# Later token sums in the expert loop, and low parts read last within each group of matmuls

## The chip, the core and the metric

The kernel runs on one core of one Trainium2 chip. Its engines are TensorE (PE in the profile, with its weight loads as PEld), VectorE (DVE), ScalarE (ACT), GpSimd (POOL) and SyncE (SP, which issues nearly all DMAs). Each works through its own instructions in the order in which the program lists them; semaphores join them. The metric is device microseconds of one execution; lower is better.

## The reference

A retention layer feeds a layer of eight experts, each token to one of them, and that feeds a two-matrix layer with an ELU:

```python
ret = (scale * q @ k.T) * Dmat; x = ret @ v           # 4 batches, 8 heads, 576 tokens, 64 wide
expert_idx = argmax(normalized(x) @ normalized(emb).T / tau)   # 2304 tokens, 8 experts
h = np.maximum(x[mask] @ w1[e], 0.0)                  # 512 -> 1024
out[mask] = gate_w[mask, None] * (h @ w2[e])          # 1024 -> 512
h = out @ w_in                                        # 512 -> 2048
g = np.where(h > 0.0, h, np.exp(np.minimum(h, 0.0)) - 1.0)
return g @ w_out                                      # 2048 -> 512
```

## The kernel before

Every matrix that goes into a matmul of the experts and of the last layer is split into a high part (rounded to fp32r, by a cast or an activation on ACT) and a low part (value minus high part, a subtraction on DVE). A product then takes three matmuls, high by high, high by low and low by high, which add into the same PSUM bank. The helper `three` issues them in that order of stationary and moving operands: weight high by data high (L224), weight high by data low (L225), weight low by data high (L226).

There are three stages. The attention stage and the sorting of tokens to experts take the first 125 us. The **expert loop** (L1144 on) has 64 iterations `i`, eight per expert, up to 366 us, and the **last layer** runs from there to the end in 24 units `n` (three blocks of 768 tokens, eight each).

One iteration of the expert loop issues `mm1(i)`, 12 matmuls of a 128-wide slice of w1 with the expert's tokens (`xth`, `xtl`) into the bank `h`; then ACT's `hh` (L879, ReLU of `h`) and DVE's `hl` (L880, the low part of the same); then `mm2(i-1)`, 12 matmuls of w2's slice with `hh` and `hl` of the iteration before, into four banks `acc0` to `acc3`. At an expert's last slice ACT copies the four banks to `ys`, and a DMA stores them to `yd` in DRAM. Beside that each iteration splits one half-megabyte piece of w1 (`ra` into `ha` and `la`, even `i`) or of w2 (`rb` into `hb` and `lb`, odd `i`) for two iterations ahead and issues the next load of it; transposes (`tp`, L853) and splits the next expert's tokens in its second half; and takes two steps (`decode(2)`) of decoding the last layer's weights: DVE's L146, L148, L151 and L154 on `draw`, ACT's square `dsq` (L149) of the same load, then a DMA of the result to `wd` and another load.

At `i = IOVER = 48`, after a branch for tokens over an expert's capacity (its body is not run here), `LY(0)` loads the first block of tokens, `yb`, 1.5 MB, from `yd`. The last layer needs seven matrices made of it. Four come from `sums(0)`, a generator of four DVE subtractions and additions of 128x768 (L1074: one rewrites a part of `yb`, three write `T`); `high(0, k)` and `low_(0, k)` then split matrix `k` (L1080 on ACT, L1086 on DVE). Before the change the four sums come one each in iterations 50 to 53, and the seven splits in 54 to 60. `decode(2)` runs in iterations up to 53. At 61 to 63 come the first unit's weights (`Sa`, `Ha`, `La`, `Hs`, `Ls`).

In the last layer `product` (L1216) issues, for the 128-row halves `kk` of a matrix, the same three matmuls each, and `unit` (L1291) the same for `fi`.

The schedule is by hand: an engine's order is that of the code. Engine orders below name tiles with a running number behind them.

Of the kernel before, what the change touches and what calls it, by code (L numbers as in the profile page):

```python
# [17 lines left out]
P = 128  # L18
# [11 lines left out]
KD = DM // P  # L30
# [49 lines left out]
def tile_kernel(ctx: ExitStack, tc: tile.TileContext, q, k, v, emb, tau, w1, w2, w_in, w_out, const, out):  # L80
    nc = tc.nc
# [26 lines left out]
    first = cp.tile([P, 1], I32, name="first")  # L108
# [9 lines left out]
    NQ = F2 // P // 2  # L118
# [93 lines left out]
    def tiles_a(i):  # L212

        o = (i % 2) * P
        return [tuple(t[:, kk * 256 + o:kk * 256 + o + P] for t in wa[i // 2]) for kk in range(KD)]

    def tiles_b(i):
        o = (i % 2) * 512
        return [tuple(t[:, o + d * P:o + d * P + P] for t in wb[i // 2]) for d in range(KD)]

    def three(o, l, r, first, last):

        (lh, ll), (rh, rl) = l, r
        nc.tensor.matmul(o, lh, rh, start=first, stop=False)  # L224
        nc.tensor.matmul(o, lh, rl, start=False, stop=False)  # L225
        nc.tensor.matmul(o, ll, rh, start=False, stop=last)  # L226

    tc_manual = ctx.enter_context(tc.manual_schedule())

# [314 lines left out]
    t = ps.tile([P, 512], F32, tag="sc0", name="warm0")  # L544
# [18 lines left out]
    t = ps.tile([P, 512], F32, tag="sc1", name="warm1")  # L563
# [99 lines left out]
    last = range(GROUPS[-1][0], NT)  # L663
# [78 lines left out]
    hi = gt[NG - 1]["hi"]  # L742
# [27 lines left out]
    fi = finish(pid, 0, 2, ids, ids0)  # L770
# [22 lines left out]
    def local(key):  # L793
        return over["pool"] if key == "x" else mp
# [4 lines left out]
    def cap(key):  # L799
        return CH if key == "x" else CAPS[key]  # L800
# [63 lines left out]
    hs = {}  # L864

    def mm1(i, key, w):
        hp = pm.tile([P, 512], F32, tag="h", name=f"h{i}", bufs=2)
        xh, xl = xt[key]
        c = cap(key)
        if i:  # L870
            for kk in range(KD):
                three(hp[:, :c], w[kk], (xh[:, kk, :], xl[:, kk, :]), kk == 0, kk == KD - 1)
        else:
            for l, r in ((0, xh), (1, xh), (0, xl)):
                for kk in range(KD):
                    nc.tensor.matmul(hp[:, :c], w[kk][l], r[:, kk, :], start=l == 0 and r is xh and kk == 0, stop=r is xl and kk == KD - 1)
        hh = local(key).tile([P, CAPS[0]], F32R, tag="hh", name=f"hh{i}")[:, :c]
        hl = local(key).tile([P, CAPS[0]], F32R, tag="hl", name=f"hl{i}")[:, :c]
        nc.scalar.activation(out=hh, in_=hp[:, :c], func=AF.Relu)  # L879
        vec.scalar_tensor_tensor(out=hl, in0=hp[:, :c], scalar=0.0, in1=hh.bitcast(F32), op0=ALU.max, op1=ALU.subtract)  # L880
        hs[i] = (hh, hl)

    acc = {}

    def mm2(i, f, key, w, ra):
        c = cap(key)
        if f == 0:
            for d in range(KD):
                acc[d] = pm.tile([P, 512], F32, tag=f"acc{d}", name=f"acc{i}_{d}")
        for d in range(KD):  # L890
            three(acc[d][:, :c], w[d], hs[i], f == 0, f == 7)
        if f == 7:
            ys = local(key).tile([P, KD, c], F32, tag="ys", name=f"ys{key}", bufs=1)
            for d in range(KD):
                nc.scalar.copy(out=ys[:, d, :], in_=acc[d][:, :c])
            nc.sync.dma_start(out=yd[:, :, bass.ds(ra(), c)], in_=ys)
# [116 lines left out]
    NI1 = NE * 8  # L1013
    IOVER = 48
# [62 lines left out]
    def high(b, k_):  # L1077
        n_ = USE[k_]
        hi, lo = (tp_["pool"].tile([P, 2, HB], F32R, tag="t" + x, name=f"{n_}{x}_{b}", bufs=10) for x in "hl")
        nc.scalar.copy(out=hi, in_=mats[b]["raw"][n_])  # L1080
        mats[b][n_] = (hi, lo)

    def low_(b, k_):
        n_ = USE[k_]
        hi, lo = mats[b][n_]
        vec.tensor_tensor(out=lo, in0=mats[b]["raw"][n_], in1=hi.bitcast(F32), op=ALU.subtract)  # L1086
# [49 lines left out]
    t = pm.tile([P, 512], F32, tag="acc1", name="warmx")  # L1136
# [7 lines left out]
    for i in range(NI1 + 1):  # L1144
        if i == IOVER - 1:
            tc.mark_branch_hint_location("rest", hint="LikelyTaken", engines=ENGS)
        if i < NI1 and i != IOVER:
            mm1(i, i // 8, tiles_a(i))
        if i:
            e, f = divmod(i - 1, 8)  # L1150
            ap = offi[0:1, e:e + 1]
            mm2(i - 1, f, e, tiles_b(i - 1), reg(nc.sync, ap, N) if e else lambda: 0)
        if i == IOVER:
            mm1(i, i // 8, tiles_a(i))
            qctx.close()
            overflow(n_trips)
            tp_["pool"] = ctx.enter_context(tc.tile_pool(name="tpool", bufs=1, side="right"))
            decode(2)
        if i == 0:
            for _ in pick(gslp, gsl):  # L1160
                pass
            gather_expert(1)
        e, f = divmod(i, 8)
        if i < NI1:
            if f == 0 and e:
                gather_expert(e + 1)
            if 4 <= f < 7:
                xpose(e + 1, f - 4)
            if 3 <= f < 6 and e + 1 < NE:
                weighs[e + 1](f - 3)  # L1170
        if i == 9:
            posf = compact()
        if 9 <= i < 21 and i % 4 == 1:
            compact_part((i - 9) // 4, posf)
        if i in (26, 27, 28):
            compact_sum(i - 26)
        if i == 28:
            compact_end()
        if i == 29:
            compact_store()  # L1180
            rest = rest_table(ord_["off"], ord_["cnp"])
        if 30 <= i < 46 and i % 2 == 0:
            next(rest, None)
        if i == 46:
            n_trips = nc.values_load(trips[0:1, 0:1], min_val=0, max_val=NK)
        if i < NI1 - 2:
            (split_b if i % 2 else split_a)(i // 2 + 1)
        if i == IOVER:
            LY(0)
            prep = sums(0)  # L1190
        if IOVER + 1 < i < IOVER + 6:
            next(prep)
        if IOVER + 6 <= i < IOVER + 13:
            high(0, i - IOVER - 6)
            low_(0, i - IOVER - 6)
        elif i < NI1 - 3 and i != IOVER - 1:
            decode(2)
        if i == NI1 - 3:
            Sa(0)
        if i == NI1 - 2:  # L1200
            Ha(0)
            La(0)
            LA(2)
        if i == NI1 - 1:
            Hs(0)
            Ls(0)
            Sa(1)
# [6 lines left out]
    acc6 = {}  # L1214

    def product(n, o, first, sl, m):  # L1216
        b = n // NQ
        hi, lo = (qa if sl in slots_a else qs)["q", n]
        o0 = (slots_a[sl] if sl in slots_a else slots_s[sl]) * 256
        mh, ml = mats[b][m]  # L1220
        for kk in range(2):
            c = slice(o0 + kk * P, o0 + kk * P + P)
            for j, (l, r) in enumerate(((hi[:, c], mh[:, kk, :]), (hi[:, c], ml[:, kk, :]), (lo[:, c], mh[:, kk, :]))):
                nc.tensor.matmul(o, l, r, start=first and kk == 0 and j == 0, stop=kk == 1 and j == 2, skip_group_check=True)  # L1224

    PR = {"P1": ("X", True, "A11", "B11"), "P6": ("Y", True, "S2", "T2"), "P2": ("X", False, "A12", "B21"), "P7": ("Y", False, "S3", "T3"),
          "P5": ("X", True, "S1", "T1"), "P4": ("Y", False, "A22", "T4"), "P3": ("X", False, "S4", "B22")}
# [63 lines left out]
    def unit():  # L1291
        if not units:
            return
        n, z, tt = units.pop(0)
        b, q_ = divmod(n, NQ)
        t = tt + 3 * (z == "B")
        if q_ == 0:
            tag = f"acc{t}" if t < 4 else "tp"
            acc6[t] = pm.tile([P, 512], F32, tag=tag, name=f"o{b}_{t}", bufs=1 if t < 4 else 2)
        bh, bl = qb["q", n]  # L1300
        gh, gl = Q[n]["gh" + z], Q[n]["gl" + z]
        for fi in range(2):
            sl, c = slice(tt * P, (tt + 1) * P), slice(fi * 512, (fi + 1) * 512)
            three(acc6[t], (gh[:, fi, sl], gl[:, fi, sl]), (bh[:, c], bl[:, c]), q_ == 0 and fi == 0, q_ == NQ - 1 and fi == 1)
        if q_ == NQ - 1:
            o_ = dec.tile([P, DM], F32 if t % 2 else I32, tag="dsq" if t % 2 else "db1", name=f"ob{b}_{t}", bufs=2)
            ob = o_ if t % 2 else o_.bitcast(F32)
            if b == 2 and t % 2:
                vec.tensor_copy(out=ob, in_=acc6[t])
            else:  # L1310
                nc.scalar.copy(out=ob, in_=acc6[t])  # L1311
            col = b * NTB + t
            pool.memset(nil, 0.0)
            ins = pool.indirect_dma_start(  # L1314
                out=out[:, :], out_offset=bass.IndirectOffsetOnAxis(ap=idc[:, col:col + 1], axis=0), in_=ob, in_offset=None)
            tc.declare_no_dep(ins.ins, group="rows", reason="each token's row is written once")
            tc.add_to_no_dep_group("rows", ins.ins)
# [29 lines left out]
    for n in range(2, QL):  # L1347
        b, q_ = divmod(n, NQ)
# [3 lines left out]
        if b < 2 and q_ == 4:  # L1352
            prep = sums(b + 1)
# [48 lines left out]
```

## Time and profile before

| what | value |
|---|---|
| median of 3 runs | 748.74 us (748.15 to 749.7) |
| the profiled execution, its own time | 748.12 us |
| its span, first to last instruction | 746.3 us |
| PE busy, share of the span | 715.5 us, 96% |
| PEld busy | 664.2 us, 89% |
| DVE busy | 577.4 us, 77% |
| ACT busy | 460.5 us, 62% |
| POOL busy | 253.6 us, 34% |

Times in the profile count from the start of the span. A matmul's row gives its start and a duration that overlaps with the following ones, so the pace of a run of matmuls is read from start to start. In brackets behind a row stands how long its engine was idle before it, and what released it. [...]

### The profile page before, as it was taken

The numbers are of one execution on the slowest core, as the hardware profiler recorded it, in microseconds if no ns is written. First come the engines' busy times: TensorE is split into PE (matmuls) and PEld (weight loads), VectorE is DVE, ScalarE is ACT, GpSimd is POOL, SyncE is SP. The second block draws the span as 40 slices with busy tenths as digits, with TensorE's granted clock in tenths as the row PEclk, the third lists the DMA queues.
The fourth block names the chain that finished last, engine by engine and source line by source line (L and its number), as shares of the span: only waits on it lengthen the run. The fifth ranks groups of instructions, "written<-read, shape, count | busy, mean of one in ns | idle before, by whom it ended". The sixth has DMA issues, their size and how long they took to land.

```text
span 746.3 us, 13522 instructions
## 1 busy us (share of the span) xinstructions
PE 715.5 (96%) x4901; PEld 664.2 (89%) x4902; DVE 577.4 (77%) x905; ACT 460.5 (62%) x716; POOL 253.6 (34%) x366
## 2 busy tenths in 40 slices
PE   8999977999999999969999999999999999999996
PEld 7998975999999999859988999989999898999995
DVE  3477767788787898668689889988778998777773
ACT  3564643565665575537576667877666787666562
POOL 4367664139931321000532132244312227211103
PEclk9999999999999999989999999999999999999999
DMA  9999955887898989778424231235222114221012
GB/s 201 232 222 236 249 164 155 267 261 262 289 310 282 323 271 325 248 267 249 139 88 138 75 96 58 84 113 171 83 72 71 57 56 164 77 71 58 28 29 84
DMA packets 126747, 123.63 MB, mean 166 GB/s; under 512 B 61738, under 2 KB 96846, under 8 KB 126678
## 3 DMA queue, kind: packets, MB, share of 16 engines
q1 hardware_dynamic: 122390, 111.67, 50.4%
q0 software_dynamic: 3104, 9.83, 3.9%
q10 hardware_dynamic: 1184, 1.24, 0.6%
q8 instruction: 39, 0.64, 0.4%
q14 instruction: 30, 0.25, 0.1%
HBM read 99.88 MB, written 22.85 MB: 164 GB/s over the span
## 4 chain that ended last, share of the span: by engine, by line
PE 25%; issue 20%; POOL 6%; DVE 4%; DMA 1%; ACT 1%; SPq 0%; POOLq 0%; DVEq 0%; ACTq 0%
PE X L1224 6%; PE Y L1224 4%; PE o L226 3%; PE o L224 3%; PE o L225 3%; POOL out_dram L1314 1%; POOL qs L1115 1%; POOL qs L1112 1%; POOL qs L1114 1%; POOL qa L1113 1%; PE acc L225 1%; DMA rb<-in_moe_w_dram 1%; PE acc L226 1%; PE acc L224 1%; PE h L224 1%
## 5 line engine op out<-in xcount | busy, mean ns | idle before, releaser
L1112 POOL TENSOR_TENSOR qs<-qa 128x256 f32<-128x256 f32 x24 | 22.4, 934 | 256.8 <-DMA qa<-wd 55.4
L225 PE MATMUL acc<-hl,hb 128*128 128x342 f32 (+7 forms) x256 | 79.0, 308 | 10.2 <-DVE hl L880 10.2
L224 PE MATMUL h<-xth,ha 128*128 128x332 f32 (+7 forms) x252 | 78.5, 312 | 1.0 <-DVEq L1022 1.0
L226 PE MATMUL acc<-hh,lb 128*128 128x342 f32 (+7 forms) x256 | 78.1, 305 | 0.0
L224 PE MATMUL acc<-hh,hb 128*128 128x342 f32 (+7 forms) x256 | 78.1, 305 | 0.0
L226 PE MATMUL h<-xth,la 128*128 128x332 f32 (+7 forms) x252 | 76.3, 303 | 0.3 <-DVE la L199 0.3
L225 PE MATMUL h<-xtl,ha 128*128 128x332 f32 (+7 forms) x252 | 76.4, 303 | 0.0
L225 PEld LDWEIGHTS acc<-hl,hb 128*128 128x128 f32 x256 | 48.8, 190 | 11.9 <-DVE hl L880 11.9
L879 ACT ACTIVATE hh<-h 128x342 fp32r<-128x342 f32 (+7 forms) x64 | 27.0, 421 | 52.3 <-PE h L226 52.0
L1266 ACT ACTIVATE rA<-hA 128x768 f32<-128x768 f32 x24 | 20.4, 848 | 55.8 <-DVE hA L1259 55.8
L1251 DVE TENSOR_TENSOR u<-Y,m 128x384 f32<-128x384 f32 x48 | 26.6, 554 | 31.6 <-PE Y L1224 29.6
L199 DVE TENSOR_TENSOR lb<-rb,hb 128x1024 fp32r<-128x1024 f32 x32 | 39.8, 1245 | 13.0 <-ACT hb L194 13.0
L199 DVE TENSOR_TENSOR la<-ra,ha 128x1024 fp32r<-128x1024 f32 x32 | 39.7, 1240 | 12.3 <-ACT ha L194 12.2
L224 PEld LDWEIGHTS h<-xth,ha 128*128 128x128 f32 x252 | 47.5, 189 | 1.6 <-DVEq L1022 1.3
L226 PEld LDWEIGHTS acc<-hh,lb 128*128 128x128 f32 x256 | 48.9, 191 | 0.0
L224 PEld LDWEIGHTS acc<-hh,hb 128*128 128x128 f32 x256 | 48.6, 190 | 0.0
L226 PEld LDWEIGHTS h<-xth,la 128*128 128x128 f32 x252 | 47.5, 189 | 0.6 <-DVE la L199 0.5
L819 POOL DMA_INDIRECT row<-xd,idsp x21 | 21.6, 1029 | 76.6 <-ACT xth L858 74.3
L225 PEld LDWEIGHTS h<-xtl,ha 128*128 128x128 f32 x252 | 47.6, 189 | 0.0
L1314 POOL DMA_INDIRECT out_dram<-ob,idc x18 | 20.3, 1127 | 68.4 <-ACT ob L1311 65.9
L194 ACT CAST hb<-rb 128x1024 fp32r<-128x1024 f32 x32 | 33.3, 1041 | 3.5 <-issue 2.2
L1259 DVE TENSOR_TENSOR hB<-X,u 128x384 f32<-128x384 f32 x48 | 26.5, 553 | 10.7 <-PE X L1224 10.4
(1684 smaller groups left out, 2390.1 us busy)
## 6 DMA issues: line engine op xcount, KB each, us to landing
ra<-in_moe_w_dram SPq DMA_DIRECT2D x31, 512.0 KB
rb<-in_moe_w_dram SPq DMA_DIRECT2D x31, 512.0 KB
qb<-wd SPq DMA_DIRECT2D x48, 256.0 KB
draw<-in_moe_w_in_dram SPq DMA_DIRECT2D x16, 512.0 KB
draw<-in_moe_w_out_dram SPq DMA_DIRECT2D x16, 512.0 KB
wd<-db SPq DMA_DIRECT2D x32, 256.0 KB
qa<-wd SPq DMA_DIRECT2D x24, 256.0 KB
qa<-wd SPq DMA_DIRECT2D x48, 128.0 KB
```

The source lines that it names most:

```text
L194: nc.scalar.copy(out=hi, in_=src)
L199: nc.vector.tensor_tensor(out=lo, in0=src, in1=hi.bitcast(F32), op=ALU.subtract)
L224: nc.tensor.matmul(o, lh, rh, start=first, stop=False)
L225: nc.tensor.matmul(o, lh, rl, start=False, stop=False)
L226: nc.tensor.matmul(o, ll, rh, start=False, stop=last)
L819: pool.indirect_dma_start(out=t[:m].rearrange("p k w -> p (k w)"), out_offset=None, in_=xd[:, :], in_offset=bass.IndirectOffsetOnAxis(ap=i ...
L879: nc.scalar.activation(out=hh, in_=hp[:, :c], func=AF.Relu)
L1112: pool.tensor_tensor(out=S1, in0=A21, in1=A22, op=ALU.add)
L1224: nc.tensor.matmul(o, l, r, start=first and kk == 0 and j == 0, stop=kk == 1 and j == 2, skip_group_check=True)
L1251: vec.tensor_tensor(out=S_[nm], in0=S_["Y"], in1=S_["m1"], op=ALU.add)
L1259: vec.tensor_tensor(out=half(n, z)[:, fi, :], in0=Q[n][bank], in1=Q[n][term], op=ALU.add)
L1314: ins = pool.indirect_dma_start(out=out[:, :], out_offset=bass.IndirectOffsetOnAxis(ap=idc[:, col:col + 1], axis=0), in_=ob, in_offset=None)
```

## The change

Two things change, and no arithmetic is added or removed.

First, within a group of matmuls that add into the same place those that read a low part made by DVE come last. `three` is gone. A new helper `several` takes all pairs of a group and issues first, for each pair, weight high with data high and weight high with data low, and behind them all the matmuls with the low weights. It serves `mm1` (whose moving low part `xtl` is old; `la` is the fresh one), `product` and `unit`. `mm2` is written out: for each `d` the high and low weights with `hh`, and behind these eight the four with `hl`. `mm1(0)` is as before.

Second, `sums(0)` comes in iterations 54 and 55, two steps each, and the seven splits come in 56 to 62. `LY(0)` and `decode` stay where they are.

```diff
-    def three(o, l, r, first, last):
-        (lh, ll), (rh, rl) = l, r
-        nc.tensor.matmul(o, lh, rh, start=first, stop=False)
-        nc.tensor.matmul(o, lh, rl, start=False, stop=False)
-        nc.tensor.matmul(o, ll, rh, start=False, stop=last)
+    def several(o, ops, first, last):
+        seq = [(lh, r) for (lh, _), rr in ops for r in rr] + [(ll, rh) for (_, ll), (rh, _) in ops]
+        for n_, (l, r) in enumerate(seq):
+            nc.tensor.matmul(o, l, r, start=first and n_ == 0, stop=last and n_ == len(seq) - 1, skip_group_check=True)
...
-            for kk in range(KD):
-                three(hp[:, :c], w[kk], (xh[:, kk, :], xl[:, kk, :]), kk == 0, kk == KD - 1)
+            several(hp[:, :c], [(w[kk], (xh[:, kk, :], xl[:, kk, :])) for kk in range(KD)], True, True)
...
+        hh, hl = hs[i]
         for d in range(KD):
-            three(acc[d][:, :c], w[d], hs[i], f == 0, f == 7)
+            for w_ in range(2):
+                nc.tensor.matmul(acc[d][:, :c], w[d][w_], hh, start=f == 0 and w_ == 0, stop=False)
+        for d in range(KD):
+            nc.tensor.matmul(acc[d][:, :c], w[d][0], hl, start=False, stop=f == 7)
...
-        if IOVER + 1 < i < IOVER + 6:
+        if i in (IOVER + 6, IOVER + 7):
             next(prep)
-        if IOVER + 6 <= i < IOVER + 13:
-            high(0, i - IOVER - 6)
-            low_(0, i - IOVER - 6)
-        elif i < NI1 - 3 and i != IOVER - 1:
+            next(prep)
+        elif IOVER + 8 <= i < IOVER + 15:
+            high(0, i - IOVER - 8)
+            low_(0, i - IOVER - 8)
+        elif i < IOVER + 6 and i != IOVER - 1:
             decode(2)
```

`product` and `unit` call `several` with their two halves in the same way.

On DVE, iterations 50 to 52 before the change: the first sum (`yb`, L1074) stands between the split of `la` and the next decode step, ahead of two low parts `hl`.

```order
L199 TENSOR_TENSOR la_5484<-ra_4842,ha_5483 128x1024
L1074 TENSOR_TENSOR yb_5394<-yb_5394 128x2x384
L146 TENSOR_SCALAR db_5503<-draw_5370 128x512
L148 SCALAR_TENSOR_TENSOR db_5503<-draw_5370,db_5503 128x512
L880 SCALAR_TENSOR_TENSOR hl_5521<-h_5507,hh_5520 128x282
L199 TENSOR_TENSOR lb_5538<-rb_4896,hb_5537 128x1024
L1074 TENSOR_TENSOR T_0_5498<-yb_5394 128x768
L151 SCALAR_TENSOR_TENSOR db_5503<-draw_5370,db_5503 128x512
L154 SCALAR_TENSOR_TENSOR db_5503<-dsq_5502,db_5503 128x512
L880 SCALAR_TENSOR_TENSOR hl_5572<-h_5558,hh_5571 128x282
```

On DVE after the change the sums stand two by two behind the splits of iterations 54 and 55:

```order
L199 TENSOR_TENSOR la_5706<-ra_5496,ha_5705 128x1024
L1076 TENSOR_TENSOR yb_5394<-yb_5394 128x2x384
L1076 TENSOR_TENSOR T_0_5720<-yb_5394 128x768
L878 SCALAR_TENSOR_TENSOR hl_5739<-h_5725,hh_5738 128x282
L199 TENSOR_TENSOR lb_5755<-rb_5546,hb_5754 128x1024
L1076 TENSOR_TENSOR T_0_5721<-yb_5394,T_0_5720 128x768
L1076 TENSOR_TENSOR T_0_5722<-yb_5394,T_0_5720 128x768
L878 SCALAR_TENSOR_TENSOR hl_5785<-h_5771,hh_5784 128x276
```

The first sum has moved behind all remaining decode steps and behind the splits and low parts of four iterations.

On PE, the group `mm2` of one iteration before the change reads `hl` in every third matmul, from the second on:

```order
L224 MATMUL acc_0_5418<-hh_4938,hb_4883 128x282
L225 MATMUL acc_0_5418<-hl_4939,hb_4883 128x282
L226 MATMUL acc_0_5418<-hh_4938,lb_4884 128x282
L224 MATMUL acc_1_5419<-hh_4938,hb_4883 128x282
L225 MATMUL acc_1_5419<-hl_4939,hb_4883 128x282
```

After it, the end of the next such group is

```order
L891 MATMUL acc_2_5420<-hh_5414,lb_4884 128x282
L891 MATMUL acc_3_5421<-hh_5414,hb_4883 128x282
L891 MATMUL acc_3_5421<-hh_5414,lb_4884 128x282
L893 MATMUL acc_0_5418<-hl_5415,hb_4883 128x282
L893 MATMUL acc_1_5419<-hl_5415,hb_4883 128x282
L893 MATMUL acc_2_5420<-hl_5415,hb_4883 128x282
L893 MATMUL acc_3_5421<-hl_5415,hb_4883 128x282
```

`hl` is read from the ninth matmul on, and the four banks are complete only with the last four.

## Rows read from the trace of the kernel before

**Rows 1.** Page, part 1: engine, busy us (share of the span), instructions.

```profile
PE 715.5 (96%) x4901; PEld 664.2 (89%) x4902; DVE 577.4 (77%) x905; ACT 460.5 (62%) x716; POOL 253.6 (34%) x366
```

**Rows 2.** Waits, whole span: engine line, waited for: us in total, times, longest.

```profile
ACT hh L879 <- PE h L226: 52.0, 33, 2.5
...
PE acc L225 <- DVE hl L880: 10.2, 7, 6.8
```

**Rows 3.** Waits of PE from 125 to 310 us.

```profile
PE acc L225 <- DVE hl L880: 2.6, 4, 0.8
...
PE h L226 <- DVE la L199: 0.3, 1, 0.3
```

**Rows 4.** Timeline of PE at 300: start, us, engine, line, operation [idle before <-releaser].

```profile
300.61 0.29 PE L224 MATMUL acc<-hh,hb 128*128 128x292 f32 x1
301.67 0.40 PE L225 MATMUL acc<-hl,hb 128*128 128x292 f32 x1 [0.77 <-DVE hl L880]
301.92 0.30 PE L226 MATMUL acc<-hh,lb 128*128 128x292 f32 x1
```

**Rows 5.** Timeline of PE, 314 to 347.

```profile
314.04 0.30 PE L224 MATMUL acc<-hh,hb 128*128 128x282 f32 x1
...
315.62 0.30 PE L224 MATMUL h<-xth,ha 128*128 128x282 f32 x1
...
317.20 0.29 PE L224 MATMUL acc<-hh,hb 128*128 128x282 f32 x1
...
324.26 0.60 PE L225 MATMUL acc<-hl,hb 128*128 128x282 f32 x1 [6.77 <-DVE hl L880]
...
326.77 0.44 PE L226 MATMUL acc<-hh,lb 128*128 128x282 f32 x1
...
330.83 0.60 PE L853 MATMUL tp<-ident,row 128*128 128x128 f32 x4
331.19 0.37 PE L224 MATMUL h<-xth,ha 128*128 128x282 f32 x1
...
347.17 0.29 PE L224 MATMUL acc<-hh,hb 128*128 128x276 f32 x1
```

**Rows 6.** Timeline of DVE, 312 to 327.

```profile
312.80 1.21 DVE L199 TENSOR_TENSOR la<-ra,ha 128x1024 fp32r<-128x1024 f32 x1
321.82 0.96 DVE L1074 TENSOR_TENSOR yb<-yb 128x768 f32<-128x768 f32 x1 [7.81 <-DMA rb<-in_moe_w_dram]
...
323.76 0.45 DVE L880 SCALAR_TENSOR_TENSOR hl<-h,hh 128x282 fp32r<-128x282 f32 x1
324.12 1.22 DVE L199 TENSOR_TENSOR lb<-rb,hb 128x1024 fp32r<-128x1024 f32 x1
325.25 0.95 DVE L1074 TENSOR_TENSOR T<-yb 128x768 f32<-128x768 f32 x1
326.12 0.68 DVE L151 SCALAR_TENSOR_TENSOR db<-draw,db 128x512 int32<-128x512 int32 x1
326.84 0.69 DVE L154 SCALAR_TENSOR_TENSOR db<-dsq,db 128x512 f32<-128x512 f32 x1
```

**Rows 7.** Windows: stretch, us, busy of each engine, PEclk, DMA share, GB/s.

```profile
324.00:325.00 1.00, 0.74 (x3) 0.74 (x4) 1.00 (x2) 0.00 (x0) 0.00 (x0) 0.50 1.06 382
325.00:326.00 1.00, 1.00 (x6) 1.00 (x5) 1.00 (x2) 0.00 (x0) 0.00 (x0) 0.50 0.46 159
```

**Rows 8.** Timeline of SP: its DMA issues, 313 to 316.

```profile
313.26 0.65 SPq L1063 DMA_DIRECT2D yb<-yd  x1
314.73 0.39 SPq L173 DMA_DIRECT2D rb<-in_moe_w_dram  x1
315.17 0.52 SPq L132 DMA_DIRECT2D draw<-in_moe_w_in_dram  x1
```

**Rows 9.** Timeline of ACT, 314 to 318.

```profile
314.91 0.67 ACT L149 ACTIVATE dsq<-draw 128x512 f32<-128x512 f32 x1 [2.50 <-DMA draw<-in_moe_w_in_dram]
315.48 0.39 ACT L879 ACTIVATE hh<-h 128x282 fp32r<-128x282 f32 x1
```

More of the change, by code (lines that the diff above doesn't have):

```diff
@@ L1220, in product @@
         mh, ml = mats[b][m]
[L1221 to L1224, printed above, removed]
+        cs = [slice(o0 + kk * P, o0 + kk * P + P) for kk in range(2)]
+        several(o, [((hi[:, c], lo[:, c]), (mh[:, kk, :], ml[:, kk, :])) for kk, c in enumerate(cs)], first, True)
     PR = {"P1": ("X", True, "A11", "B11"), "P6": ("Y", True, "S2", "T2"), "P2": ("X", False, "A12", "B21"), "P7": ("Y", False, "S3", "T3"),
@@ L1301, in unit @@
         gh, gl = Q[n]["gh" + z], Q[n]["gl" + z]
-        for fi in range(2):
-            sl, c = slice(tt * P, (tt + 1) * P), slice(fi * 512, (fi + 1) * 512)
-            three(acc6[t], (gh[:, fi, sl], gl[:, fi, sl]), (bh[:, c], bl[:, c]), q_ == 0 and fi == 0, q_ == NQ - 1 and fi == 1)
+        sl = slice(tt * P, (tt + 1) * P)
+        several(acc6[t], [((gh[:, fi, sl], gl[:, fi, sl]), (bh[:, fi * 512:(fi + 1) * 512], bl[:, fi * 512:(fi + 1) * 512])) for fi in range(2)],
+                q_ == 0, q_ == NQ - 1)
         if q_ == NQ - 1:
```

## The prediction

> **What bounds the kernel now.** I read the page's busy shares first. PE is busy 96% of the span [rows 1], so the end is set by PE's work and by the gaps in it, and this change takes no matmul away. Next the waits of the whole span: PE's largest entry by far is the low part `hl` made by DVE, 10.2 us in seven waits, one of them 6.8 us [rows 2]. Four of the seven, 2.6 us, lie before 310 us, with one wait of 0.3 us for `la` [rows 3]. The other direction is longer: ACT waited 52.0 us for PE's bank `h` [rows 2]. ACT and DVE follow PE in the expert loop, so PE time won there is not lost again to a slower engine.
>
> Then the long wait, on three engines. DVE ends the split `la` at 314.0 and stands idle for 7.81 us before the first sum [rows 6]. The releaser is given as the load of `rb`, but the sum reads `yb`; `yb` was issued at 313.26 and `rb` right behind it [rows 8], and the two are not told apart there. Behind the sum stand, in DVE's order, the decode steps and `hl`, which starts at 323.76 [rows 6]. PE reaches the group `mm2` that reads this `hl` at 317.20, gets one matmul out, and resumes at 324.26 [rows 5]. [...]
>
> **The early waits.** The example [rows 4] shows what one costs. The second matmul starts 1.06 us after the first, where the undisturbed pace is about 0.13 (twelve matmuls in 1.58 us [rows 5]): 0.93 us lost, and the next start comes 0.25 after it instead of 0.13, so 1.05 us in all. The idle column gives 0.77 for it. The difference, 0.28, is the overlap of a matmul's row with its follower and the restart. [...] By the idle column alone this term would be 2.9 us.
>
> From start to start the five early waits are 2.6 + 0.3 + 5 x 0.28 = 4.3 us. The new order makes `hl` due at the ninth matmul of the group instead of the second, seven matmuls or 0.93 us later, and `la` at the ninth instead of the third, 0.8 us later. The four waits for `hl` average 0.65 idle and the example, the longest, is just covered. I take 4.2 us; the lower end is 2.9.
>
> **The long wait.** Between 317.20 and 347.17 [rows 5] pass 29.97 us. In them lie twelve groups of twelve matmuls (`mm2` of iterations 51 to 56, `mm1` of 53 to 58). Eight are 282 columns wide at 1.58 us [rows 5]; four are 276 wide, which scales to 1.55. With three transpose groups of 0.36 (330.83 to 331.19 [rows 5]) that is 12.6 + 6.2 + 1.1 = 19.9 us of work. So 10.1 us are lost here: 6.93 at the wait (7.06 from start to start, less 0.13), some 1.3 at half clock (ten matmuls take 2.51 us from 324.26 to 326.77 [rows 5] instead of 1.3, and the first few later ones), and the rest in two later waits for `hl`, behind further sums. With the sums in iterations 54 and 55 `yb` has long landed and DVE passes from `la` straight to the decode step; the `hl` that came at 323.76 needs only `hh`, which ended near 315.9 [rows 9], and a `draw` that had landed by 314.91 [rows 9]; it comes near 316.5, before PE asks at 317.3, even without the new order.
>
> What is late next? Two things, and they are costs of this term.
>
> The **load behind `yb`**. The decode load `draw` of 315.17 is queued behind `yb` and `rb` [rows 8]. The transfers are saturated until 325 and thin out in the next microsecond [rows 7]. That `draw` lands between 323.2 (0.5 MB behind the landing of `rb` or `yb` near 321.8, at 382 GB/s [rows 6, 7]) and 325.4. Before the change nobody met it: everyone stood still. Now ACT's next `dsq` waits for it, and in ACT's order `hh` of iteration 53 stands behind that `dsq`. From the landing it takes 0.57 (start of `dsq` to start of `hh` [rows 9]) plus 0.4. PE has four groups of 1.58 and two transposes of 0.36 to do from 317.20 before it asks for that `hh`, which is 324.25. Landing at 324.3, the middle, gives `hh` at 325.4 and a wait of 1.15 us. The ends are 0 and 2.3.
>
> The **sums in their new place**. In iterations 54 and 55 DVE does, from start to start, two splits at 1.13, four sums at 0.87 to 0.95, the last two decode steps (0.72 + 0.6) and two `hl` at 0.36 [rows 6], about 8.1 us, against 2 x 3.16 = 6.3 of PE [rows 5]. It falls 1.8 behind, of which the new order covers 0.93: 0.85 us lost. The ends are 0 and 1.8, as if there were no cover. From 56 on DVE has a split, a low part and `hl`, 2.4 us for 3.1 of PE, and recovers.
>
> So this term is 10.1 - 1.15 - 0.85 = 8.1 us, between 6.0 and 10.1.
>
> **What I cost at nothing.** The seven splits end in iteration 62 instead of 60; their first reader is the last layer, and the load of the first unit's weights moves up with the loop. Behind 366 us the waits view names no low part for PE, so the order in `product` and `unit` wins nothing. An expert's four banks are now complete with the ninth to twelfth matmul instead of the third to twelfth, so ACT's copies to `ys` begin 0.8 us later, once per expert. ACT has the room (52.0 us of waiting [rows 2]) and the next use of the banks lies a whole `mm1`, 1.6 us or more, behind; without that cover it would be up to 0.8 us in each of eight experts. The pace of a matmul by its neighbours: a group `mm2`, with four banks, takes 314.04 to 315.62, and `mm1`, with one bank, 315.62 to 317.20 [rows 5], the same within 0.01 us in twelve, or 1 ns each. The change reorders some 3,400 matmuls (756 + 768 in the loop, 1,008 + 864 in the last layer), so 1 ns each would be 3.4 us either way; I take 0.
>
> **The sum.** 4.2 + 8.1 = 12.3 us. Against the profiled execution, 748.12, that is 735.8; this execution lies 0.6 below the median of the runs, 748.74, so I forecast 736.4. The ends of the terms give 8.9 to 14.4, that is 739.8 to 734.3.
>
> **The rivals.** First, **the wait is handed on**: the loads behind `yb` come at the late end or later, ACT stands at `dsq` or at the cast of `rb`, the later `ys` copies push ACT further, and the sums in 54 and 55 find DVE already late. Then the second term is 6.0 less some 2 to 3 for an ACT that stays behind over an expert's end, and the first is 2.9: a gain of 6 to 7, near 742. For it speaks the saturated stretch [rows 7]; against it that at most the one `draw` is due before 326. [...] 14%.
>
> Second, **the change misses the cause**: the first sum waits not for `yb` but for something that also comes late in iteration 54, as the named releaser `rb` would allow. The 7.8 us then come back there, softened by 0.9 of cover: a gain of 4.2 + 1.5, near 743. Against it: `rb` of 314.73 is itself split in iteration 53, ahead of the sum's new place. 4%.
>
> Third, **slower**: repeated stationary operands. Before, each group of three starts with two matmuls on the same weights; in `mm2` now no two neighbours share them. If a load of new weights showed between matmuls, 4 of 12 matmuls in 64 groups, 256, would pay. A weight load's row is busier than the matmul pace leaves room for (664.2 us for 4,902, 0.136 us each [rows 1], against 0.132). The loss must pass 12.3 / 256 = 48 ns each to decide; at 60 ns it is 15.4 us and the time 751.8. Against it: in each group before, the third matmul already changes the weights, and it starts no later than the second (a whole group of twelve keeps 0.132 [rows 5]). 4%.
>
> **How the numbers follow.** The forecast has 74%: 736.4, with 733.5 to 740 for its bounds and a little for the pace. Handed on 14%, cause missed 4%, slower 4%, and 4% for a gain above 15 us, where PE running ahead also removes stalls that the idle column hides. To leave out no more than 2 in 10 the range takes in the forecast and the larger part of the first rival: 733.5 to 741.5. A measurement of this kernel can tell about 0.2%, 1.5 us, from no change. Faster by more than that: 0.92; within it 0.04 (parts of the second rival and of the first, with a pace lost in the last layer); slower 0.04.
>
> **What would show it.** In the profile after: no wait of PE above 3 us in the expert loop and PEclk at 1.00 through the stretch around 310 to 340; DVE's first sum with no wait for a DMA; a new wait of ACT's `dsq` for `draw` of about 3 us, and of PE for `hh` of about 1; waits for `hl` below 1 us in total; a start of the last layer about 12 us earlier, and the same length of it. It is wrong if the last layer becomes longer (pace), if PE still waits several us for `hl` (cause), or if the early waits reappear under the name of `hh` or `lb`.

## The result and the profile after

The kernel after the change takes 740.91 us (median of 4 runs, 739.2 to 742.63) against 749.22 for the kernel before in the same comparison (4 runs, 748.15 to 750.05): a ratio of 0.989, with an interval from 0.986 to 0.992. That is 8.3 us; the forecast was 12.3 us and 736.4, with a range up to 741.5. The profiled execution after took 739.2 us with a span of 737.4, 8.9 us shorter than the span before.

The busy shares answer to [rows 1], and the second row, of the waits view, to the 52.0 us of [rows 2]: PE's work is what it was, and ACT waits 10 us less for `h`.

```profile
PE 714.9 (97%) x4902; PEld 662.6 (90%) x4902; DVE 579.2 (79%) x905; ACT 458.5 (62%) x716; POOL 255.3 (35%) x366
```

```profile
ACT hh L877 <- PE h L225: 42.4, 32, 2.3
```

Then the waits of PE in the expert loop. This is the waits view of PE over the whole span after (engine line, waited for: us in total, times, longest); the entries left out lie before the loop, at its edges or, one of 0.7, in the last layer.

```profile
PE acc L891 <- ACT hh L877: 2.2, 2, 2.0
...
PE h L225 <- DVEq L1024: 1.0, 1, 1.0
...
PE acc L891 <- DVE lb L199: 0.3, 1, 0.3
```

The 10.2 us for `hl` [rows 2] and the early waits [rows 3] are gone; 0.3 us of them came back under the name of `lb`. New is a wait for `hh`, 2.2 us. The timeline of PE shows where. First two rows of before that stand nowhere above (the restart at the branch of iteration 48, the last layer's first matmul):

```profile
306.04 0.40 PE L224 MATMUL h<-xth,ha 128*128 128x282 f32 x1 [1.04 <-DVEq L1022]
365.51 0.34 PE L1224 MATMUL X<-B11h,ha('q', 0)_6083 128*128 128x384 f32 x1
```

The same places after, and between them the first matmul of `mm2` in iterations 51 to 54 and 57 (314.53 answers to 317.20 and 338.00 to 347.17 of [rows 5]):

```profile
302.97 0.40 PE L225 MATMUL h<-xth,ha 128*128 128x282 f32 x1 [1.04 <-DVEq L1024]
314.53 0.40 PE L891 MATMUL acc<-hh,hb 128*128 128x282 f32 x1 [0.26 <-ACT hh L877]
318.45 0.29 PE L891 MATMUL acc<-hh,hb 128*128 128x282 f32 x1
324.17 0.40 PE L891 MATMUL acc<-hh,hb 128*128 128x282 f32 x1 [1.97 <-ACT hh L877]
328.24 0.29 PE L891 MATMUL acc<-hh,hb 128*128 128x282 f32 x1
338.00 0.29 PE L891 MATMUL acc<-hh,hb 128*128 128x276 f32 x1
356.59 0.34 PE L225 MATMUL X<-B11h,ha('q', 0)_6083 128*128 128x384 f32 x1
```

From these starts the 8.9 us can be divided by stretch:

The loop's first matmul started at 122.68 before and at 123.08 after; work ahead of the loop is the same in both.

| stretch | before, us | after, us | gain | forecast |
|---|---|---|---|---|
| to the loop's first matmul | 122.68 | 123.08 | -0.40 | 0 |
| to the restart at the branch | 183.36 | 179.89 | 3.47 | 4.2 |
| to `mm2` of iteration 51 | 11.16 | 11.56 | -0.40 | 0 |
| to `mm2` of iteration 57 | 29.97 | 23.47 | 6.50 | 8.1 |
| to the last layer | 18.34 | 18.59 | -0.25 | 0 |
| the last layer, to the span's end | 380.8 | 380.8 | 0 | 0 |

The sums no longer wait for anything, and the clock stays up. The first is DVE's first sum after (it answers to 321.82 in [rows 6]); the second a part of the windows (stretch, us, busy of PE, PEld, DVE, ACT, POOL, then PEclk, the clock granted to TensorE as a share of full speed, DMA share, GB/s).

```profile
330.28 0.95 DVE L1076 TENSOR_TENSOR yb<-yb 128x768 f32<-128x768 f32 x1
```

```profile
308.00:310.00 2.00, 2.00 (x17) 2.00 (x16) 1.97 (x5) 1.33 (x2) 0.00 (x0) 1.00 0.00 0
312.00:314.00 2.00, 2.00 (x18) 2.00 (x16) 0.00 (x0) 0.48 (x1) 0.00 (x0) 1.00 1.02 353
324.00:326.00 2.00, 1.82 (x12) 1.58 (x12) 1.97 (x4) 2.00 (x4) 0.00 (x0) 1.00 1.06 406
```

PEclk is 1.00 where it was 0.50 before [rows 7]. The DMA column tells something new: the transfers are empty at 308 to 310 (share 0.00) and full from 312 on (1.02 and more up to 328). What PE now waits for is on ACT and SP:

```profile
313.52 0.67 ACT L149 ACTIVATE dsq<-draw 128x512 f32<-128x512 f32 x1 [4.19 <-DMA draw<-in_moe_w_in_dram]
323.16 0.66 ACT L149 ACTIVATE dsq<-draw 128x512 f32<-128x512 f32 x1 [3.94 <-DMA draw<-in_moe_w_in_dram]
323.72 0.39 ACT L877 ACTIVATE hh<-h 128x282 fp32r<-128x282 f32 x1
```

```profile
309.37 0.41 SPq L132 DMA_DIRECT2D draw<-in_moe_w_in_dram  x1
311.94 0.65 SPq L1065 DMA_DIRECT2D yb<-yd  x1
...
313.85 0.75 SPq L132 DMA_DIRECT2D draw<-in_moe_w_in_dram  x1
```

The `draw` issued at 313.85, behind `yb`, is used at 323.16, the moment it lands; `hh` of iteration 53 stands behind its square on ACT; PE resumes 0.45 after `hh` began. The mechanism is the one forecast. Its price is not.

### The profile page after: what moved, and what is told of

It reads as the page before. It is cut to its first block, busy times and chain, and to the rows that moved or that the text cites. A ratio compares the mean times of both kernels' runs of the same rounds, so it can differ in the third digit from the quotient of the medians.

```text
span 737.4 us, 13518 instructions
## 1 busy us (share of the span) xinstructions
PE 714.9 (97%) x4902; PEld 662.6 (90%) x4902; DVE 579.2 (79%) x905; ACT 458.5 (62%) x716; POOL 255.3 (35%) x366
## 4 chain that ended last, share of the span: by engine, by line
PE 35%; issue 9%; DVE 8%; ACT 2%; DMA 2%; POOL 1%; POOLq 0%; SPq 0%; ACTq 0%; DVEq 0%
PE o L225 16%; PE X L225 9%; PE Y L225 7%; PE h L225 1%; PE acc L891 1%; DMA ra<-in_moe_w_dram 1%; PE acc L893 1%; POOL out_dram L1315 1%; DVE hA L1280 1%; DVE glA L1288 1%; DVE xA L1277 1%; DMA draw<-in_moe_w_in_dram 1%; DVE hB L1280 0%; DVE la L199 0%; DVE xB L1277 0%
## 5 line engine op out<-in xcount | busy, mean ns | idle before, releaser
L891 PE MATMUL acc<-hh,hb 128*128 128x342 f32 (+7 forms) x256 | 73.7, 304 | 2.2 <-ACT hh L877 2.2
L225 PE MATMUL h<-xth,ha 128*128 128x332 f32 (+7 forms) x252 | 74.3, 311 | 1.0 <-DVEq L1024 1.0
L891 PE MATMUL acc<-hh,lb 128*128 128x342 f32 (+7 forms) x256 | 73.6, 303 | 0.3 <-DVE lb L199 0.3
L225 PE MATMUL h<-xtl,ha 128*128 128x332 f32 (+7 forms) x252 | 72.2, 303 | 0.0
L199 DVE TENSOR_TENSOR la<-ra,ha 128x1024 fp32r<-128x1024 f32 x32 | 39.1, 1222 | 11.6 <-ACT ha L194 11.5
L893 PE MATMUL acc<-hl,hb 128*128 128x342 f32 (+7 forms) x256 | 47.1, 306 | 0.1
L225 PE MATMUL h<-xth,la 128*128 128x332 f32 (+7 forms) x252 | 45.6, 303 | 0.0
L893 PEld LDWEIGHTS acc<-hl,hb 128*128 128x128 f32 x256 | 38.8, 188 | 1.4 <-DVE hl L878 1.0
L225 PEld LDWEIGHTS h<-xth,la 128*128 128x128 f32 x252 | 38.5, 189 | 0.0
L1260 DVE TENSOR_TENSOR hB<-X,u 128x384 f32<-128x384 f32 x48 | 26.6, 553 | 10.7 <-PE X L225 10.4
```

Of the source, the lines that this page charges most:

```text
L199: nc.vector.tensor_tensor(out=lo, in0=src, in1=hi.bitcast(F32), op=ALU.subtract)
L225: nc.tensor.matmul(o, l, r, start=first and n_ == 0, stop=last and n_ == len(seq) - 1, skip_group_check=True)
L891: nc.tensor.matmul(acc[d][:, :c], w[d][w_], hh, start=f == 0 and w_ == 0, stop=False)
L893: nc.tensor.matmul(acc[d][:, :c], w[d][0], hl, start=False, stop=f == 7)
L1260: vec.tensor_tensor(out=half(n, z)[:, fi, :], in0=Q[n][bank], in1=Q[n][term], op=ALU.add)
```

## Experiments

All ratios are against the kernel before in the same comparison; its medians there were 749.0 to 749.7.

**The two parts apart.** One kernel has only the moved sums, one only the new order.

```diff
 # e1_sums_only: the kernel before, with
-        if IOVER + 1 < i < IOVER + 6:
+        if i in (IOVER + 6, IOVER + 7):
+            next(prep)
             next(prep)
-        if IOVER + 6 <= i < IOVER + 13:
+        elif IOVER + 8 <= i < IOVER + 15:
...
```

> The kernel before with the four sums moved to iterations 54 and 55 and the splits to 56 to 62, every matmul in its old order. My theory (the sums' place removes the 6.8 us wait, the order of the matmuls removes the small early ones): the five early waits for hl and la stay (2.9 us idle), the long one is gone and PEclk stays at 1.00 near 310 to 340; in its place ACT waits some 3 us for draw, PE about 1 us for hh of iteration 53, and hl is late in 54 to 56 by up to 1.8 us in all since nothing covers it. Gain 6 to 8 us, near 742. Rival (the whole gain of 8.3 us comes with the order of the matmuls): no gain, near 749.

Measured: 743.6 us (740.39 to 745.89, 6 runs), ratio 0.9913 (0.9893 to 0.9934), a gain of 6.1. The moved sums find `yb` landed; PE (first row) and ACT (second) show what came instead, and the windows the clock behind it:

```profile
328.30 0.55 PE L224 MATMUL acc<-hh,hb 128*128 128x282 f32 x1 [2.72 <-ACT hh L879]
```

```profile
327.29 0.66 ACT L149 ACTIVATE dsq<-draw 128x512 f32<-128x512 f32 x1 [4.69 <-DMA draw<-in_moe_w_in_dram]
```

```profile
328.00:330.00 2.00, 0.94 (x2) 0.63 (x3) 1.93 (x4) 2.00 (x4) 0.00 (x0) 0.60 1.04 398
330.00:332.00 2.00, 2.00 (x10) 2.00 (x10) 1.86 (x3) 0.56 (x2) 0.00 (x0) 0.50 0.60 214
```

The wait for the `draw` behind `yb` belongs to the moved sums; it needs no early gain. It is longer than forecast, and behind it the clock falls here, which was not expected. The profiled execution, 745.89 us, is the longest of the six.

```diff
 # e2_order_only: the changed kernel, with
-        if i in (IOVER + 6, IOVER + 7):
-            next(prep)
+        if IOVER + 1 < i < IOVER + 6:
             next(prep)
-        elif IOVER + 8 <= i < IOVER + 15:
+        if IOVER + 6 <= i < IOVER + 13:
...
```

> The changed kernel with the four sums back in iterations 50 to 53 and the splits in 54 to 60, every matmul in its new order. My theory: PE has gained 3.5 us at the start of iteration 49, but SP's issue of yb after the branch moves up by only 1.3 us and DVE still stands until yb lands, so most of the lead is lost at the long wait, which becomes longer in idle time (about 8 us less 0.9 of cover); the two hl waits behind it go (1.3 us). Gain 3 to 4 us, near 745.5. Rival (the two parts add up, each on its own path): the gain is that of the whole less that of the sums alone, and the long wait stays at 6 us or below.

Measured: 745.58 us (743.61 to 746.22, 6 runs), ratio 0.9942 (0.9926 to 0.9958), a gain of 4.2, as expected. PE and DVE:

```profile
302.94 0.40 PE L225 MATMUL h<-xth,ha 128*128 128x282 f32 x1 [1.04 <-DVEq L1024]
322.56 1.31 PE L893 MATMUL acc<-hl,hb 128*128 128x282 f32 x4 [7.30 <-DVE hl L878]
```

```profile
320.13 0.96 DVE L1076 TENSOR_TENSOR yb<-yb 128x768 f32<-128x768 f32 x1 [9.21 <-DMA rb<-in_moe_w_dram]
```

PE passes the branch 3.10 us earlier than before (306.04), but `yb` is used only 1.69 earlier (320.13 against 321.82 in [rows 6]). The long wait becomes longer, 7.30 instead of 6.8, although the new order covers seven matmuls more. In this execution, the longest of the six, only 1.92 of the 3.10 us are left at the last layer (363.59). One reason is the clock: PE works at half clock (PEclk 0.50) from 322.56 to about 328.2, before only from 324.26 to about 327.5. The parts gain 6.1 and 4.2 alone, 10.3 together; the whole gains 8.3 to 8.9. The intervals are too wide to tell these sums apart; that the parts share a limit is shown by the rows, where most of the lead is lost at the load.

**The order in the last layer alone.**

```diff
 # e4_last_layer_order: the kernel before, with `several` added and used in `product` and `unit` only
-            for j, (l, r) in enumerate(((hi[:, c], mh[:, kk, :]), (hi[:, c], ml[:, kk, :]), (lo[:, c], mh[:, kk, :]))):
-                nc.tensor.matmul(o, l, r, start=first and kk == 0 and j == 0, stop=kk == 1 and j == 2, skip_group_check=True)
+        several(o, [((hi[:, c], lo[:, c]), (mh[:, kk, :], ml[:, kk, :])) for kk, c in enumerate(cs)], first, True)
...
```

> The kernel before with the new order of matmuls in the last layer alone (product and unit); the expert loop is untouched. My theory: no low part is waited for there and the pace of a matmul does not depend on its neighbours, so no change, within 0.7 us of the kernel before, and the last layer lasts 380.8 us as before. Rival (the order changes the pace, by 1 ns or more on each of 1,872 matmuls): 1.9 us or more to either side.

Measured: 748.89 us (748.03 to 750.04, 11 runs), ratio 0.9991 (0.998 to 1.0003): no difference that can be told. With the equal length of the last layer in the table above, the rival on weight loads and pace falls, there and, by the undisturbed groups of the loop (304.64 to 307.79 for 24 matmuls after, 3.15 us, against 3.16 before), in `mm2` too.

**The load behind the others.** `LY(0)` goes to the end of iteration 49, behind that iteration's `rb` and `draw`.

```diff
 # e3_load_behind: the changed kernel, with
-        if i == IOVER:
-            LY(0)
-            prep = sums(0)
...
+        if i == IOVER + 1:
+            LY(0)
+            prep = sums(0)
```

> The changed kernel with the load yb issued an iteration later, behind the loads of rb and draw of iteration 49 instead of ahead of them; nothing else moves. My theory (what is left of the loss is ACT waiting for a draw that lies behind 1.5 MB of yb): ACT's second wait for draw (3.9 us) and PE's wait of 2.0 us for hh of iteration 53 go, the first one (4.2 us of ACT, 0.3 us of PE) stays, and the first sum still finds yb landed: 2 to 3 us less than the changed kernel, near 738.3. Rival (the loss is DVE's crowd of sums in 54 and 55, or SP's late start after the branch): the wait of PE moves to another name and the time stays within 0.7 us of the changed kernel's.

Measured: 738.13 us (736.37 to 739.8, 5 runs), ratio 0.9849 (0.9829 to 0.987), as expected and better than both kernels. SP, ACT and PE:

```profile
313.36 0.42 SPq L132 DMA_DIRECT2D draw<-in_moe_w_in_dram  x1
...
314.57 0.65 SPq L1065 DMA_DIRECT2D yb<-yd  x1
```

```profile
321.12 0.66 ACT L149 ACTIVATE dsq<-draw 128x512 f32<-128x512 f32 x1 [1.30 <-DMA draw<-in_moe_w_in_dram]
```

```profile
315.15 0.40 PE L891 MATMUL acc<-hh,hb 128*128 128x282 f32 x1 [0.19 <-ACT hh L877]
331.73 0.78 PE L893 MATMUL acc<-hl,hb 128*128 128x282 f32 x4 [0.38 <-DVE hl L878]
```

With `yb` behind it the `draw` lands 7.76 us after its issue instead of 9.31, PE's wait of 1.97 is gone, and `yb`, not needed before iteration 54, is still in time. From the restart (303.65) to the last layer's first matmul (355.52) pass 51.87 us instead of 53.62 in the changed kernel.

**Why the load is late: SP's place or full transfers.** Between the store of `yd` and the next `draw` SP issues nothing for 7.14 us in the changed kernel (302.23 to 309.37), of which it spends 4.9 in the branch of iteration 48. Two kernels leave that branch out.

```diff
 # e8_before_no_branch: the kernel before; e7_after_no_branch: the changed kernel; both with
-            overflow(n_trips)
```

> The kernel before without the branch (left out; its body is not run here). Same theory: yb is issued about 4 us earlier against TensorE, so VectorE's wait at the first sum falls from 7.81 to about 4 us and TensorE's wait for hl from 6.8 to about 3 us, and with a shorter wait the half clock behind it may be gone. Gain 1.04 + 4 and up to 1.3 for the clock: 742.5 to 745. Rival, the load is late by the transfers and not by the issue: the long wait stays at 6 us or more and the time is about 748.

Measured: 746.91 us (745.33 to 748.1, 9 runs), ratio 0.996 (0.9946 to 0.9975), a gain of 2.6. SP, DVE and PE:

```profile
310.86 0.62 SPq L1063 DMA_DIRECT2D yb<-yd  x1
```

```profile
320.35 0.96 DVE L1074 TENSOR_TENSOR yb<-yb 128x768 f32<-128x768 f32 x1 [6.61 <-DMA yb<-yd]
```

```profile
322.79 0.60 PE L225 MATMUL acc<-hl,hb 128*128 128x282 f32 x1 [6.36 <-DVE hl L880]
```

`yb` goes out 2.40 us earlier than at 313.26 [rows 8] and is used 1.47 earlier; PE, free of the branch, comes earlier too, and still waits 6.36 instead of 6.8. So this is nearer to the rival: the issue moved by only 2.40 us, not 4, of which 1.47 came through. The run bears on another point: the sum's releaser is named `yb` here.

> The changed kernel without the branch for tokens over an expert's capacity (left out; its body is not run here). If SyncE's stay of some 4.8 us in that branch is what makes the loads behind it late against TensorE, SP's first draw and the load of yb go out about 4 us earlier against TensorE (yb then has to wait for the store of yd to land, some 6 us), ACT's wait of 3.94 us at the second dsq falls below 1 us, the first one falls too, and TensorE's two waits for hh (0.52 and 2.23 from start to start) go. Together with the 1.04 us that TensorE itself waits at the branch that is a gain of 3.8 us on the changed kernel, about 737.1. Rival, the loads are late because the transfers are full wherever SP issues them: only the 1.04 is won, about 739.9, and TensorE still waits 1.5 to 2 us for hh.

Measured: 735.72 us (735.13 to 736.89, 4 runs), ratio 0.9809 (0.9789 to 0.9829). SP, ACT and PE, and two windows:

```profile
308.24 0.63 SPq L1065 DMA_DIRECT2D yb<-yd  x1
...
310.19 0.49 SPq L132 DMA_DIRECT2D draw<-in_moe_w_in_dram  x1
```

```profile
320.93 0.66 ACT L149 ACTIVATE dsq<-draw 128x512 f32<-128x512 f32 x1 [3.70 <-DMA draw<-in_moe_w_in_dram]
```

```profile
321.93 0.40 PE L891 MATMUL acc<-hh,hb 128*128 128x282 f32 x1 [1.73 <-ACT hh L877]
```

```profile
308.00:310.00 2.00, 2.00 (x18) 2.00 (x17) 1.97 (x4) 0.86 (x3) 0.00 (x0) 1.00 1.09 328
320.00:322.00 2.00, 0.27 (x3) 0.07 (x1) 0.33 (x1) 1.07 (x3) 0.00 (x0) 1.00 1.08 417
```

The `draw` goes out 3.66 us earlier, at 310.19, and is used 2.23 earlier, 10.7 us after its issue instead of 9.3. The hole in the transfers at 308 to 310 is filled and PE's first wait for `hh` gone, as the first theory said; the second wait stays, 1.73 us, as the rival said. By medians the gain on the changed kernel is 5.2, above either figure; by the two profiled spans (737.4 and 735.0) it is 2.4, between them. The two traces are far from typical: one is the shortest of its four runs (739.2 to 742.63), the other the longest (735.13 to 736.89). All four runs without the branch lie below both 737.1 and 739.9, so the time speaks for the first theory and the wait that stays for the rival.

**A queue of its own for `yb`.**

```diff
 # e6_pool_queue: the changed kernel, with
-            nc.sync.dma_start(out=yb, in_=yd[:, :, b * TB:(b + 1) * TB])
+            (nc.sync if b else nc.gpsimd).dma_start(out=yb, in_=yd[:, :, b * TB:(b + 1) * TB])
```

> The changed kernel with the load of yb issued by GpSimd, on a queue of its own, in the same place of the code. Theory (the second draw is late because it is queued behind yb, and yb is late because SP issues it behind its branch): yb goes out as soon as the store of yd has landed, some 3 us earlier; ACT's wait at the second dsq falls from 3.94 to below 2.5 us and TensorE's wait for hh of 1.97 to below 0.5; the first draw now shares the transfers with yb, and TensorE's first wait for hh (0.26) may grow to 1.5. Time 737 to 740. Rival (full transfers, whatever the queue): ACT still waits 4 us or more at one of the two, and the sum of TensorE's waits for hh stays at 2 us or more: 741.

Measured: 741.83 us (741.44 to 742.9, 4 runs), ratio 0.9897 (0.9876 to 0.9918): the rival's case. POOL, ACT and PE:

```profile
309.71 0.82 POOL L1065 DMA_DIRECT2D yb<-yd  x1 [12.60 <-DVE db L154]
```

```profile
324.57 0.66 ACT L149 ACTIVATE dsq<-draw 128x512 f32<-128x512 f32 x1 [2.12 <-DMA draw<-in_moe_w_in_dram]
```

```profile
322.50 0.41 PE L225 MATMUL h<-xth,ha 128*128 128x282 f32 x1 [1.82 <-ACT ha L194]
325.57 0.40 PE L891 MATMUL acc<-hh,hb 128*128 128x282 f32 x1 [1.03 <-ACT hh L877]
```

No longer behind `yb` in a queue, the `draw` of 312.95 lands 11.6 us after its issue, later than in the changed kernel, and `ra`, the load that `ha` is made of, is late as well. So to stand behind `yb` in its queue is not what it takes to be late; to be in flight together with it was enough here (11.62 us against 9.31). `ra`, issued at 310.85 with `yb` already out, is used 10.55 us later; the `ra` of 311.19 in the changed kernel, issued ahead of `yb`, was there when ACT came to it after 7.00.

**More in front of the branch, and `yb` in parts.** Both start from the version with the load behind.

```diff
 # e9_decode_ahead: e3_load_behind, with the two decode steps behind the branch in iteration 47 instead
             overflow(n_trips)
-            decode(2)
...
-        elif i < IOVER + 6 and i != IOVER - 1:
+        elif i < IOVER + 6:
             decode(2)
```

> The changed kernel with the load of yb behind the other loads of iteration 49, and the first two decode steps behind the branch moved to iteration 47, ahead of it, so that the first draw is issued ahead of SP's branch too. Theory: ACT's wait of 4.1 us at the dsq of iteration 50 goes, TensorE's remaining wait for hh (0.2) too; the time falls by at most 0.5 us from 738.1, to 737.6 to 738.1. Rival: the two steps on VectorE ahead of the branch make hl of iteration 48 later and TensorE waits up to 0.5 us more there: 738.6.

Measured: 740.65 us (738.97 to 741.38, 4 runs), ratio 0.9881 (0.986 to 0.9902): no gain, rather a loss of some 2 us, more than the rival said and by another way. PE:

```profile
327.81 0.40 PE L225 MATMUL h<-xth,ha 128*128 128x276 f32 x1 [1.29 <-ACT ha L194]
```

The early wait for `draw` is gone, but PE meets the next late load, `ra`, and later waits 0.66 for `lb`. The loads behind the branch have fallen back against PE: the first of `ra` goes out 8.70 us after PE's restart (302.73 to 311.43) instead of 7.72 in the version with the load behind (303.65 to 311.37).

```diff
 # e10_four_parts: e3_load_behind, LY(0) making the tile only, and
+        if IOVER < i < IOVER + 5:
+            k_ = i - IOVER - 1
+            nc.sync.dma_start(out=tp_["yb"][:, k_, :], in_=yd[:, k_, :TB])
```

> The changed kernel with the load of yb cut into four parts of 384 KB, issued at the ends of iterations 49 to 52, each behind the other loads of its iteration. Theory: the limit is the transfers. The loop by itself asks for one ra, one rb and one draw of 512 KB and one wd of 256 KB in two iterations of some 6.3 us, about 285 GB/s; the trace shows some 390 GB/s when the transfers are full; four parts in 12.6 us add about 125 GB/s, so they just fill them. No load of the loop then stands behind more than one part: ACT's waits for draw stay below 2 us except for the first one behind SP's branch, no wait of TensorE in iterations 50 to 56 is above 0.5 us, the sums find yb landed, and the time is 737 to 738.1, like the version with the whole load behind the others (738.1) or a little better. Rival, the number of issues on SP or the later parts count: the sums in iteration 54 wait for the last part, TensorE waits 1 us or more for hl, and the time is 739 to 741.

Measured: 742.44 us (740.49 to 744.83, 6 runs), ratio 0.9911 (0.9889 to 0.9933). The theory's figure missed. DVE, PE and the windows:

```profile
331.41 0.96 DVE L1079 TENSOR_TENSOR yb<-yb 128x768 f32<-128x768 f32 x1 [3.59 <-DMA yb<-yd]
```

```profile
333.78 0.78 PE L893 MATMUL acc<-hl,hb 128*128 128x282 f32 x4 [3.73 <-DVE hl L878]
```

```profile
330.00:332.00 2.00, 0.05 (x1) 0.00 (x0) 0.59 (x1) 0.00 (x0) 0.00 (x0) 1.00 1.03 398
334.00:336.00 2.00, 2.00 (x12) 2.00 (x12) 2.00 (x3) 1.79 (x5) 0.00 (x0) 0.66 0.11 39
```

No wait of PE is left in iterations 50 to 53, as the theory said; but the last part, issued at 322.25, lands at about 331.4, and the sums and PE wait for it, as the rival said; the time is above the rival's 739 to 741 too. The transfers stay full until 332: the backlog is larger than the estimate of 285 GB/s for the loop allowed.

## Why the prediction was right, and where its sum was off

The direction and both mechanisms held; the size did not, and that the range took in the result is in part luck. The gain of 8.3 us is below the slow end of the sum's own terms, 8.9 (739.8 us). The range reached to 741.5 because it made room for the first rival, and two of the four runs (741.93 and 742.63) lie above even that. What bounds the kernel, that ACT and DVE follow PE, and that the early waits are for `hl` and `la`: confirmed by the order alone (e2). That the long wait is for `yb`: confirmed by the moved sums (e1) and by the releaser in e8; the rival that the cause is missed falls. Pace and weight loads: nothing, by e4 and by the last layer's equal length. Of the sign list, no wait above 3 us, PEclk, the sum without a wait, `dsq`'s wait of about 3 us (3.94), and the missing `hl` all came; "hh about 1 us" (1.97) and "12 us earlier" (8.9) did not.

**The early waits, 4.2 forecast, 3.47 measured.** About 0.3 is `lb`, the next fresh split, which the new order lets PE reach sooner. The rest is the overlap of 0.28, read off one wait and given to all five. By the starts of the groups `mm2`, before less after, the five iterations with a wait gain 0.45 (with the wait for `lb` in it), 0.46, 0.89, 0.55 and 0.94: 3.29 together, little above the 2.9 of the idle column.

**The long wait, 8.1 forecast, 5.85 measured** (the stretches from the restart to the last layer: -0.40 + 6.50 - 0.25). The step that failed is the term for the load behind `yb`, 1.15 us with ends at 0 and 2.3. In the changed kernel the stretches from `mm2` of iteration 51 to that of 54 take these times beyond their work of 3.52 (two groups and a transpose): 0.40 (314.53 to 318.45), 2.20 (to 324.17), 0.55 (to 328.24). With the 0.40 ahead of 314.53 the draw waits cost 3.55, three times the term (3.15 if the same stretches of e10, where PE waits in none of them, are taken for the work). The moment of landing was forecast well: from issue to use pass 9.31 us (313.85 to 323.16), which on the issue of before, 315.17, gives 324.5; I had 324.3. What was wrong is the other side. I took the moment at which PE asks, 324.25, from the trace of before, and counted the early gain as a separate term. But that gain moves PE ahead by 3.07 at the restart, and the load only by 1.32: SP issued it at 313.85 instead of 315.17. The difference, 1.75, is lost again where PE needs the loads: 0.40 of it at a first `draw`, issued late behind SP's branch at 309.37, the rest at the second. The order alone shows the same thing (PE 3.10 ahead, `yb` 1.69). Term and difference make 2.90 of the 3.55. Of the 0.65 that remain 0.55 lie in the stretch behind the second wait, where `hl` is late as well as `hh`. The decode step that stands ahead of this `hl` in DVE's order waited too, and the sum had no term for that:

```profile
323.93 0.43 DVE L146 TENSOR_SCALAR db<-draw 128x512 int32<-128x512 int32 x1 [3.22 <-DMA wd<-db]
```

Its releaser is the store of an earlier result to `wd`, issued at 314.65, behind `yb` like the `draw`. (The sum has a slip beside this, without weight: 324.3, 0.57 and 0.4 make 325.27, not 325.4.)

**The sums in their new place, 0.85 forecast**, cost 0.39 (from `mm2` of iteration 55 at 331.38 to 338.00 pass 6.62 us for 6.23 of work). The working counted the last two decode steps, 1.3 us, into iterations 54 and 55; they stand ahead of them (the last begins at 328.02, the first sum at 330.28). Without them DVE falls behind by about 0.5, less than the cover of 0.93. That PE lost 0.39 all the same fits a DVE that comes late out of the stretch before; no run shows this apart.

So what happened lies between the forecast and its first rival: ACT stands at `dsq`, as the rival has it, but not because the load came later than forecast; PE came earlier. Why the loads don't follow PE has two parts, and which is the larger isn't shown. SP's stay in the branch is one (without it the `draw` lands 2.2 us earlier). The other is that the transfers are full from 312 to 328 or later in the changed kernel (DMA share 1.02 to 1.07): no queue, place or cutting of `yb` made all loads timely; each moved the wait to another reader. Place counts all the same. ACT waits for the `draw` of iteration 52 in every run with the sums moved, so its landing can be read: issued behind `yb` it takes 9.31 us (after), 11.00 (e1) and 10.74 (e7), beside `yb` on another queue 11.62 (e6), ahead of it 7.76 (e3), 6.43 (e9) and 7.57 (e10). How the engines share the bytes among loads in flight stays open. Open as well is how much of the run-to-run spread of 3 us behind a median belongs to waits at this place. The profiled execution after is the shortest of its four. The mean granted clock of the two shorter ones is 0.994, that of the two longer ones 0.991 and 0.990; so the longer ones may hold a stretch at half clock that the profiled one has not, which no trace shows.

## What to carry to other kernels

Terms that lie one behind the other on the same engine don't add when something between them keeps its own time. Here the earlier gain moved PE by 3.07 us and the load that it met next by 1.32; so work out the later wait with the engine's new time and the load's old one. When a stall is taken away, look at the transfer share of the stretch behind it: here the stall was also the time in which the transfers emptied (share 1.06 at 324 to 325 before, then 0.46 [rows 7]; 1.06 and 1.04 from 324 to 328 after). A large load that is not needed soon goes behind the small ones that are; here that was worth 2.8 us more by medians (738.13 against 740.91, with runs that overlap slightly), while cutting it up (742.44) or giving it a queue of its own (741.83) was worth nothing.

## What was not expected of the hardware

TensorE's clock fell behind a wait of 2.72 us (e1: PEclk 0.60 in 328 to 330, then 0.50 until 335; one matmul and a further wait of 0.76 followed the wait) and behind one of 3.73 us (e10: 0.66 in 334 to 336), but not behind those of 1.97 us (after) and 1.73 us (e7), where it stayed at 1.00. So the wait of e1 cost some 3 us beyond its own length, an estimate: about 6.8 us at half speed from 328.4 on, in some 6 of which PE had work.

SP's way through the branch whose body is not run takes long here. The waits view of SP after shows it:

```profile
SPq L1024 <- SPq L1024: 5.4, 2, 4.9
```

4.9 us of the 7.14 between the store of `yd` (302.23) and the next issue (309.37) pass there, while PE waits 1.04 us at the same branch. Without the branch (e7) the gap is 1.6 us (301.94 to 303.54). What SP does in the 4.9 us the trace does not tell apart, so the cause of its stay is not shown.
